# Attention and two MoE layers on one core: the bias table row by row, own buffers for one pass, and new planner costs

## The chip, the cores and the metric

The kernel runs on one core of one Trainium2 chip. Its time is the device time of one execution in microseconds (us); lower is better. The core has TensorE (PE) for matmuls, VectorE (DVE), ScalarE (ACT), GpSimd (POOL), and SyncE (SP), whose queue issues most of the DMAs. Each engine works through its own queue in order and waits on semaphores for the others.

## The reference, cut to what matters

```
B, H, S, D = 4, 8, 576, 64
scores = q @ k.T / sqrt(D)                       # per batch and head
x      = log1p(|i - j|) / log1p(max(i, 1))       # i, j: positions
bias   = maximum(x * w1 + b1, 0) @ w2            # S x S x H, the same for every batch
attn   = softmax(scores + bias[h]);  o = attn @ v
x      = o as [2304, 512]
h      = max(x @ w1, x @ w2, x @ w3);  x = h @ w_out          # first MoE,  d_ff  768
out    = (sigmoid(x @ w_gate) * (x @ w_val)) @ w_out          # second MoE, d_ff 1536
```

Inputs and outputs are float32; the MoE weights come in as 64-bit floats and are decoded on the chip. The kernel splits numbers into a high and a low float16 part and makes three matmuls (high-high, high-low, low-high) of one product.

## The kernel before

**Bias.** The table of all biases, bias_d, lies in device memory, [H, S, S + 64] in float32, head by head. It is made in 36 groups of 16 rows (`bias_rows`): four hidden tiles on ACT or DVE, 16 small matmuls, an eviction on ACT or DVE (`copy_psum`, L574 and L575) into one of three staging buffers, and one store of 320 KB on the SP queue (L661). Partition p of a staging buffer holds one row of one head, row by row and in a row head by head.

**Attention.** `pair(P, it)` works on heads 2P and 2P + 1 (modulo 8) of batch P // 4 and on query block it: 128 rows each for it = 0 to 3 and 64 rows for it = 4. It loads the biases of these rows and the two heads (L815 on SP or L816 on ACT), makes the scores (L804, L807), adds and takes the maximum on DVE (L820), and the exponential on ACT (L821). `by_pe` normalizes on POOL (L831) or DVE (L832) and transposes on PE (L836); `by_dma` does it by DMA transposes (L847). `value_out` multiplies with v (L863). In the first batch the loop goes over query blocks outside and heads inside, and the remaining bias groups are made in between: after the first query block 24 of the 36 groups are recorded, after the second 32, after the third all. So the bias stage and the first batch of attention run together.

**First MoE.** `moe1(b)` makes the products of batch b with three weight matrices (L914). For batch 0 it goes in two passes, over tokens 0 to 255 and 256 to 575. In a pass it goes through the three matrices, and in each through six columns of 128 features. A column is 12 matmuls into one of two PSUM banks in turn (`mm_0`, banks 6 and 7). A column of the first matrix is evicted into one of six column buffers `hms` (L574, L575), those of the second and third take the maximum with it (L944), and after the third the buffer is split into hT (L950, L951). The first three `hms` lie in the room `hm_f` of tile wm, the second three in tile x, at X2[:, 5760:6912]. The weights are read and decoded by a side job (`first_weights`): loads L674, decode in three DVE steps (L536 to L538), split into float16 on ACT (L684) and DVE (L685). For the output weights its raw buffers are X2[:, 3072:4608] and X2[:, 4608:6144] in turn.

**Second MoE.** After attention, its weights and staging take over the room of tile am (`attic`), and L914 and L1179 fill PE to the end.

**Order.** Everything is first recorded, with the regions that it reads and writes, and then `emit` plans one order for each engine: a list scheduler with a window per engine, four classes of priority (bias and MoE evictions first, then attention, the MoE, preparations) and an estimate of each instruction's duration (`cost`). An item that may run on two engines goes where it would end first. The planner follows every region exactly; for its dependences on the chip, the framework below it finds them again by its own means and puts in the semaphore waits. The order in a queue is then fixed.

Of the kernel before, what the change touches and what calls it, by code (L numbers as in the profile page):

```python
# [10 lines left out]
F32 = mybir.dt.float32  # L11
# [110 lines left out]
class Recorder:  # L122
# [8 lines left out]
    def __init__(self, nc, untracked):  # L131
        self.nc = nc
        self.untracked = untracked
        self.items, self.first = [], 0
        self.mem = Mem()
        self.cls = 0
        self.joined = None
        self.t_eng = {e: 0.0 for e in self.WINDOW}
        self.busy = {e: 0.0 for e in self.WINDOW}
        self.t_dma = 0.0  # L140
        self.bank = {i: {} for i in range(8)}
        self.log = []
        self.passed = {e: False for e in self.WINDOW}
        for attr, eng in self.ENGINES.items():
            setattr(self, attr, Engine(self, getattr(nc, attr), eng))
# [51 lines left out]
    @staticmethod  # L197
    def cost(eng, method, out, reads, kwargs):

        n = 1  # L200
        for _, c in out.ap[1:]:
            n *= c
        parts = out.ap[0][1]
        psum = any("PSUM" in str(a.space) for a in reads)
        if method.startswith("dma"):
            if "transpose" in method:
                return 1.33 if n > 1200 else 1.0 + 0.0003 * n, 0.12 + 0.00141 * n, 1.6
            dram = "DRAM" in str(out.space)
            if dram:
                n, parts = 1, 1  # L210
                for _, c in out.ap:
                    n *= c
            size = n * parts * (4 if "32" in str(out.dtype) else 2)
            return (0.45 if eng == "SP" else 0.1), size / (285e3 if dram else 400e3 if size > 6e5 else 300e3) * (1.6 if parts == 64 and n > 500 else 1.0) + 0.03, 1.85
        if eng == "PE":
            f32 = "float32" in str(reads[0].dtype)
            if method == "transpose":
                return 0.045 + 0.00055 * n, 0.0, 0.22
            if n <= 8:
                return 0.142, 0.0, 0.22  # L220
            t = (max(n / 2400, 0.03) + 0.0023) * (4 if f32 else 1)
            if kwargs.get("tile_position") is not None:
                depth = reads[0].ap[0][1]
                t *= (depth if depth < 128 else parts) / 128
                t += 0.012 if f32 else 0.008 if depth < 128 else 0.004
                if n <= 64:
                    t += 0.012
            return t, 0.0, 0.22
        vec = any(isinstance(kwargs.get(x), bass.AP) for x in ("scale", "bias")) or any(a.ap[-1][1] == 1 and n > 8 for a in reads)
        if eng == "DVE":  # L230
            half = "16" in str(out.dtype) and all("16" in str(a.dtype) for a in reads)
            if n <= 8:
                return (0.1 if n <= 2 else 0.13), 0.0, 0.12
            add = 0.07 if vec else 0.0
            t = {"tensor_tensor_reduce": 0.07 + 0.00105 * n, "scalar_tensor_tensor": 0.055 + 0.00107 * n + add,
                 "tensor_scalar": 0.07 + add + 0.00104 * n if psum or half else 0.03 + 0.0006 * n + add, "tensor_tensor": 0.065 + 0.00106 * n,
                 "tensor_copy": 0.08 + (0.00063 if not psum else 0.00105) * n, "memset": 0.1 + 0.0005 * n}[method]
            return t, 0.0, 0.12
        if eng == "ACT":
            t = (0.08 if psum else 0.19 if method != "copy" else 0.1) + (0.09 if psum and vec else 0.0) + 0.00083 * n  # L240
            return t + (0.09 if "accum_out" in kwargs and vec else 0.01), 0.0, 0.14
        t = {"tensor_tensor": 0.3 + 0.002 * n, "tensor_scalar": 0.08 + 0.00112 * n, "tensor_copy": 0.08 + 0.00112 * n}.get(method, 0.1 + 0.003 * n)
        if method == "tensor_scalar" and kwargs.get("op1") == ALU.max:
            t = 2.2
        return t, 0.0, 0.12

    def start(self, it, e):

        t = self.t_eng[e]
        for d in it.deps:  # L250
            e2, lat, own = self.ends[d]
            x = own if e2 == e == "PE" else lat
            if x > t:
                t = x
        for i in it.banks:
            for o, x in self.bank[i].items():
                if o != e and x > t:
                    t = x
        return t

    def choose(self, e, lists, force=False):
# [31 lines left out]
    def emit(self):  # L293

        items, by_k = self.items, {it.k: it for it in self.items}
        self.ends = getattr(self, "ends", {})
        lists = {e: [[] for _ in range(self.NCLS)] for e in self.WINDOW}
        for it in items:
            it.left = 0
            for d in it.deps:  # L300
                if d in by_k:
                    by_k[d].users.append(it)
                    it.left += 1
            for e in it.alts:
                lists[e][it.cls].append(it)
        left = len(items)
        picks = {}
        stale = set(lists)
        while left:
            for e in stale:  # L310
                picks[e] = self.choose(e, lists)
            cand = [(p[0], e) for e, p in picks.items() if p]
            if not cand:
                picks = {e: self.choose(e, lists, True) for e in lists}
                cand = [(p[0], e) for e, p in picks.items() if p]
            s, e = min(cand)
            it = picks[e][1]
            calls, (busy, work, lat) = it.alts[e]
            self.t_eng[e] = s + busy
            self.busy[e] += busy  # L320
            if work:
                self.t_dma = max(self.t_dma, s + 0.3) + work
                f = self.t_dma + lat
                self.ends[it.k] = (None, f, f)
            else:
                self.ends[it.k] = (e, s + busy + lat, s + busy)
                for i in it.banks:
                    self.bank[i][e] = s + busy + lat
            self.log.append((s, busy, e, it.k, it.cls))
            it.done = True  # L330
            left -= 1
            stale = set(it.alts) | {e}
            for u in it.users:
                u.left -= 1
                if not u.left:
                    stale |= set(u.alts)
            stale |= {o for o in lists if self.passed[o] or picks[o] and (len(picks[o][1].alts) > 1 or picks[o][1].banks & it.banks)}
            for o, ks in lists.items():
                if o in stale:
                    for c in range(self.NCLS):  # L340
                        if ks[c] and ks[c][0].done:
                            ks[c] = [x for x in ks[c] if not x.done] if len(ks[c]) < 64 else self.trim(ks[c])
            for c in calls:
                c()
        self.first += len(items)
        self.items = []
# [91 lines left out]
def tile_kernel(ctx, tc, q, k, v, w1, b1, w2, mw1, mw2, mw3, mwo, gw, vw, ow, xtab, masks, out):  # L438
    B, H, S, D = q.shape
# [6 lines left out]
    HS, SB = S // 2, S + 64  # L446
# [6 lines left out]
    junk = const.tile([128, 768], BF16, tag="junk", name="junk")  # L453
    nc = Recorder(tc.nc, {x.tensor.name for x in (junk[:, :], q, k, v, w1, b1, w2, mw1, mw2, mw3, mwo, gw, vw, ow, xtab, masks, out)})

    bias_d = dram.tile([H, S, SB], F32, tag="bias_d", name="bias_d")
    PS = psum.tile([128, 4096], F32, tag="ps", name="ps")

    def bank(i, n=512, at=0):
# [8 lines left out]
    Am = arena.tile([128, NA], F32, tag="am", name="am")  # L468
# [3 lines left out]
    def take(mem, n):  # L472
        a = free[id(mem)]
        free[id(mem)] = a + n
        return mem[:, a:a + n]

    def ring(mem, count, n, view=lambda x: x):
        return Ring([view(take(mem, n)) for _ in range(count)])
# [22 lines left out]
    ph_at = free[id(Am)]  # L501
    ph_r = ring(Am, 2, 2 * S, lambda t: t.bitcast(F16).rearrange("p (a s) -> p a s", a=2))
    e_r = ring(Am, 2, 2 * S)
    PT0 = take(Am, 2304)
    PT1 = take(Am, 2880)
    pt0 = PT0.rearrange("p (t s) -> p t s", t=9)
# [135 lines left out]
    def bias_rows(ti):  # L642
# [15 lines left out]
        m_ = msk[:, 4 + ti:5 + ti]  # L658
        copy_psum(bsb[:, 64:576], bo, m_)
        copy_psum(bsb.rearrange("p (a s) -> p a s", a=2)[:, :, 0:64], bt.unsqueeze(1).to_broadcast([128, 2, 64]), m_)  # L660
        nc.sync.dma_start(bias_d[:, 16 * ti:16 * ti + 16, :].rearrange("h i j -> i h j"), bsb[:, 0:SB])  # L661


    def first_weights(mats, raw, home, squares):
# [144 lines left out]
    def pair(P, it):  # L809

        m, h0 = rows[it], 2 * P % H
        e, l, r, bt = e_r(), l_r(), r_r(), bias_r()
        src = bass.AP(tensor=bias_d.tensor, offset=(h0 * S + 128 * it) * SB + 64, ap=[[SB, m], [S * SB - 64, 2], [1, S]])
        with nc.join():
            nc.sync.dma_start(bt[:m].rearrange("p (o s) -> p o s", o=2), src)  # L815
            nc.scalar.dma_start(bt[:m].rearrange("p (o s) -> p o s", o=2), src)  # L816
# [112 lines left out]
    def moe1(b, xd, mm):  # L929
# [27 lines left out]

        if b == 0:
            mm_0 = [mm, mm]
            hms = [t[:, 320 * i:320 * (i + 1)] for t in (hm_f, X2[:, 5760:6912]) for i in range(3)]  # L960
            for hf in range(2):
                for wi in range(3):
                    for m in range(K1):
# [278 lines left out]
```

## Time and profile before

| | us |
|---|---|
| median of 3 runs | 1083.62 |
| lowest, highest | 1081.85, 1084.55 |
| the profiled execution | 1084.82 |
| its span, first to last instruction | 1083.0 |
| PE busy | 1019.7 (94%) |
| DVE busy | 635.3 (59%) |
| ACT busy | 552.3 (51%) |
| POOL busy | 130.3 (12%) |
| mean granted TensorE clock | 0.979 |

Busy is the time in which an engine runs at least one instruction. The granted clock is the share of TensorE's full clock, 2.4 GHz; the lower of its two levels is 1.2 GHz. In the views an instruction is named by its line (L914), and tiles by their names without numbers: am, wm and x are the three large on-chip rooms, ps is PSUM, bias_d the table in device memory. A wait is put down to what released it last.

### The profile page before, as it was taken

How to read it: one execution, taken by the hardware profiler on the slowest of the kernel's cores; microseconds unless marked ns; L12 is line 12 of the kernel's file. 1: busy time of each engine (PE TensorE's matmuls, PEld its weight loads, DVE VectorE, ACT ScalarE, POOL GpSimd, SP SyncE). 2: the span in 40 equal slices, each digit the busy share in tenths (PEclk: the TensorE clock that was granted, in tenths of full speed). 3: DMA queues.
4: the chain of work that ended last, by engine and by line, in shares of the span. 5: the costliest groups of instructions: out<-in, count | busy, mean ns of one | idle time of the engine just before them, and what ended most of it. 6: DMA issues, size and time to landing. Idle time of an engine off the chain costs nothing.

```text
span 1083.0 us, 20927 instructions
## 1 busy us (share of the span) xinstructions
PE 1019.7 (94%) x8232; PEld 685.9 (63%) x8232; DVE 635.3 (59%) x1576; ACT 552.3 (51%) x1159; POOL 130.3 (12%) x159
## 2 busy tenths in 40 slices
PE   5877897799999999999999999999999999999998
PEld 2343465466566666676678777777765666776643
DVE  5866887788787887878899947922221221212210
ACT  6877896678788877777666426522110111211100
POOL 1011223503120422211110000000000000000000
PEclk9989898889999999999999999999999999999999
DMA  7767675978998989969855421000000000000001
GB/s 224 210 202 232 209 221 167 246 162 197 228 232 184 234 220 203 206 136 237 160 162 156 154 81 40 20 2 1 10 11 21 19 10 10 11 11 10 11 20 39
DMA packets 181133, 132.96 MB, mean 123 GB/s; under 512 B 123308, under 2 KB 152236, under 8 KB 181036
## 3 DMA queue, kind: packets, MB, share of 16 engines
q1 hardware_dynamic: 177364, 124.26, 46.0%
q10 hardware_dynamic: 3672, 7.38, 2.3%
q8 instruction: 64, 1.05, 0.4%
q14 instruction: 33, 0.27, 0.1%
HBM read 89.53 MB, written 16.52 MB: 98 GB/s over the span
## 4 chain that ended last, share of the span: by engine, by line
PE 79%; DVE 8%; DMA 6%; ACT 4%; issue 2%; POOL 1%; SPq 0%; ACTq 0%; POOLq 0%; DVEq 0%
PE ps L914 46%; PE ps L1179 13%; PE ps L863 6%; PE ps L804 4%; PE ps L836 4%; PE ps L650 2%; DMA bias_d<-am 2%; PE ps L807 2%; DMA am<-in_q_dram 1%; DVE am L820 1%; ACT am L574 1%; POOL am L831 1%; DMA am<-am 1%; PE ps L548 1%; DVE wm L944 1%
## 5 line engine op out<-in xcount | busy, mean ns | idle before, releaser
L914 PE MATMUL ps<-wm 128*128 128x320 f16 (+2 forms) x2304 | 305.1, 286 | 3.3 <-DVE wm L944 2.9
L914 PEld LDWEIGHTS <-am 128*128 128x128 f16 x2304 | 225.5, 98 | 58.8
L914 PEld LDWEIGHTS <-wm 128*128 128x128 f16 x2304 | 222.8, 99 | 60.3 <-issue 8.8
L914 PE MATMUL ps<-x,am 128*128 128x288 f16 x1728 | 214.3, 286 | 0.0
L821 ACT ACTIVATE am<-am,small 128x576 f32<-128x576 f32 (+1 forms) x160 | 123.0, 770 | 43.9 <-DVE small L820 37.7
L1179 PE MATMUL ps<-wm 128*128 128x512 f16 x648 | 142.0, 379 | 0.0
L1153 DVE SCALAR_TENSOR_TENSOR wm<-ps,wm 128x576 f32<-128x576 f32 x48 | 36.4, 757 | 161.6 <-PE ps L914 160.4
L820 DVE CUSTOM_DVE_ANT_0 am<-ps,am 128x576 f32<-128x576 f32 (+1 forms) x160 | 117.6, 748 | 22.4 <-issue 5.5
L1150 ACT ACTIVATE wm<-ps,ug 128x576 f32<-128x576 f32 x48 | 35.6, 741 | 155.0 <-PE ps L914 154.8
L1179 PEld LDWEIGHTS <-wm 128*128 128x128 f16 x648 | 63.4, 98 | 74.0
L1154 ACT CAST wm<-wm 128x576 f16<-128x576 f32 x48 | 32.2, 671 | 129.4 <-DVE wm L1153 129.4
L863 PE MATMUL ps<-am 128*64 128x320 f16 (+3 forms) x1000 | 88.4, 323 | 6.9 <-DVE small L594 4.5
L831 POOL TENSOR_SCALAR am<-am,small 128x576 f32<-128x576 f32 (+1 forms) x73 | 70.2, 971 | 198.1 <-DVE small L823 118.5
L836 PE MATMUL ps<-ident,am 128*128 128x128 f32 x396 | 66.5, 290 | 11.1 <-POOL am L831 7.5
L914 PE MATMUL ps<-am 128*128 128x288 f16 x576 | 71.2, 286 | 0.0
L574 ACT ACTIVATE am<-ps 128x512 f32<-128x512 f32 (+3 forms) x128 | 58.5, 473 | 15.3 <-PE ps L836 13.8
L1184 DVE TENSOR_TENSOR am<-ps,uo 128x512 f32<-128x512 f32 x16 | 11.1, 692 | 93.3 <-PE ps L1179 93.3
L845 DVE SCALAR_TENSOR_TENSOR am<-am,small 128x576 f16<-128x576 f32 (+1 forms) x72 | 59.2, 847 | 10.3 <-ACT am L844 9.7
L836 PEld LDWEIGHTS ps<-ident,am 128*128 128x128 f32 x396 | 45.7, 146 | 28.2 <-POOL am L831 15.3
L804 PE MATMUL ps<-am 64*128 64x512 f16 (+1 forms) x390 | 57.0, 389 | 3.2 <-DVE small L820 3.1
L581 ACT ACTIVATE junk<-am 128x640 bf16<-128x640 f32 (+1 forms) x72 | 48.8, 678 | 20.2 <-DVE am L538 8.9
L863 PEld LDWEIGHTS ps<-am 128*64 128x64 f32 x640 | 41.9, 150 | 22.7 <-issue 8.9
(148 smaller groups left out, 1181.1 us busy)
## 6 DMA issues: line engine op xcount, KB each, us to landing
am<-bias_d SPq DMA_DIRECT2D x52, 576.0 KB, 4.4
bias_d<-am SPq DMA_DIRECT2D x36, 320.0 KB, 3.5
wm<-in_moe_w_dram SPq DMA_DIRECT2D x12, 768.0 KB, 5.5
am<-bias_d ACTq DMA_DIRECT2D x12, 576.0 KB, 4.4
am<-in_moe_w_gate_dram SPq DMA_DIRECT2D x12, 512.0 KB, 4.6
am<-in_moe_w_val_dram SPq DMA_DIRECT2D x12, 512.0 KB, 4.6
am<-in_moe_w_out_dram SPq DMA_DIRECT2D x12, 512.0 KB, 3.4
out_dram<-am SPq DMA_DIRECT2D x36, 128.0 KB, 2.3
```

The lines of the kernel that those rows point to most:

```text
L574: nc.scalar.activation(dst, src, AF.Copy, scale=scale)
L581: nc.scalar.activation(junk[:, 0:n], src, AF.Square, accum_out=acc)
L804: nc.tensor.matmul(s_main[o][:m], lhsT=q_[h, eq], rhs=k_[h, ek, 0:512], start=(i == 0), stop=(i == 2), tile_position=(64 * o, 0))
L820: nc.vector.tensor_tensor_reduce(e[:m, c], S_[o][:m], bt[:m, c], -1.0, 3.0e38, ALU.add, ALU.min, mx[:m])
L821: nc.scalar.activation(e[:m, c], e[:m, c], AF.Exp, scale=-1.0, bias=mx[:m], accum_out=l[:m, o:o + 1])
L831: nc.gpsimd.tensor_scalar(e[:m, c], e[:m, c], r[:m, o:o + 1], 1.0, op0=ALU.mult, op1=ALU.mult)
L836: nc.tensor.transpose(ps[:, t], e[:, 128 * (t0 + t):128 * (t0 + t) + 128], ident)
L845: nc.vector.scalar_tensor_tensor(ph[:m, 1, c], e[:m, c], f, ph[:m, 0, c], op0=ALU.mult, op1=ALU.subtract)
L863: nc.tensor.matmul(ps[64 * o:64 * o + 64, :N], lhsT=vv[:, o, tv], rhs=pp[:, tb], start=(i == j == 0), stop=(i == len(todo) - 1 and j == 4) ...
L914: nc.tensor.matmul(ps, lhsT=W(wp, kk), rhs=X(xp, kk), start=(first and i == 0), stop=(last and i == 2))
L1153: nc.vector.scalar_tensor_tensor(hm3(sg), pv, DOWN2, hm3(sg), op0=ALU.mult, op1=ALU.mult)
L1179: nc.tensor.matmul(po, lhsT=gT[:, gi, kk, 128 * ct:128 * ct + 128], rhs=OW[:, wi, kk], start=(kk == 0 and i == 0), stop=(kk == K2 - 1 and ...
```

## The change

Three things are changed together. The bias table becomes [S, H, S + 64]: row by row, the eight heads of a row side by side, so that a store is one contiguous block, and a load reads for each row one run of 1152 values over two neighbouring heads. (In a table row the 64 places at one end are a copy, so that the even head is read from place 64 and the odd head from place 0.) The second three column buffers of the first MoE's first batch get 960 columns of their own in tile am, ahead of the two buffers of transposed probabilities, which move up. And the planner's durations are set anew: DMA transposes and SP's issue of a DMA take longer, PE's small products and POOL's scaling too, and a DMA can start no earlier than the eighth DMA before it has landed.

```diff
+        self.lanes = [0.0] * 8
...
-                return 1.33 if n > 1200 else 1.0 + 0.0003 * n, 0.12 + 0.00141 * n, 1.6
+                return (1.55 if n > 1200 else 1.1 + 0.0003 * n), 0.12 + 0.00141 * n, 1.6
...
-            return (0.45 if eng == "SP" else 0.1), size / ...
+            return (0.55 if eng == "SP" else 0.1), size / ...
...
-                t += 0.012 if f32 else 0.008 if depth < 128 else 0.004
+                t += 0.012 if f32 else 0.012 if depth < 128 else 0.006
...
-        t = {..., "tensor_scalar": 0.08 + 0.00112 * n, "tensor_copy": 0.08 + 0.00112 * n}...
+        t = {..., "tensor_scalar": 0.09 + 0.0014 * n, "tensor_copy": 0.09 + 0.0014 * n}...
...
+        if it.alts[e][1][1]:
+            t = max(t, self.lanes[0])
...
+                self.lanes = self.lanes[1:] + [f]
...
-    bias_d = dram.tile([H, S, SB], F32, tag="bias_d", name="bias_d")
+    bias_d = dram.tile([S, H, SB], F32, tag="bias_d", name="bias_d")
...
+    hm_x = take(Am, 960)
     PT0 = take(Am, 2304)
...
-        nc.sync.dma_start(bias_d[:, 16 * ti:16 * ti + 16, :].rearrange("h i j -> i h j"), bsb[:, 0:SB])
+        nc.sync.dma_start(bias_d[16 * ti:16 * ti + 16].rearrange("i h j -> (i h) j"), bsb[:, 0:SB])
...
-        src = bass.AP(tensor=bias_d.tensor, offset=(h0 * S + 128 * it) * SB + 64, ap=[[SB, m], [S * SB - 64, 2], [1, S]])
+        src = bass.AP(tensor=bias_d.tensor, offset=(128 * it * H + h0) * SB + 64, ap=[[H * SB, m], [SB - 64, 2], [1, S]])
...
-            hms = [t[:, 320 * i:320 * (i + 1)] for t in (hm_f, X2[:, 5760:6912]) for i in range(3)]
+            hms = [t[:, 320 * i:320 * (i + 1)] for t in (hm_f, hm_x) for i in range(3)]
```

## Rows read from the trace of the kernel before

**Rows 1.** Windows by stretch: busy us (x instructions) of each engine, clock, DMA.

```profile
core 0: us, PE busy (x) PEld busy (x) DVE busy (x) ACT busy (x) POOL busy (x), PEclk, DMA share, GB/s
0.00:40.00 40.00, 24.69 (x243) 12.44 (x243) 26.00 (x67) 27.41 (x46) 4.47 (x14) 0.96 0.81 228
40.00:166.00 126.00, 106.57 (x1087) 56.96 (x1086) 94.60 (x250) 101.26 (x218) 23.44 (x27) 0.93 0.70 216
166.00:226.00 60.00, 44.53 (x347) 27.60 (x345) 45.71 (x131) 37.84 (x96) 23.32 (x24) 0.80 0.68 175
226.00:613.00 387.00, 379.06 (x3268) 266.88 (x3266) 325.79 (x844) 285.43 (x639) 77.58 (x94) 1.00 0.85 196
613.00:1083.00 470.00, 464.80 (x3296) 321.99 (x3296) 143.19 (x287) 100.38 (x164) 1.53 (x1) 1.00 0.08 22
```

**Rows 2.** Chain of waits, 40 to 110 us: shares by line, then start, us, what.

```profile
by line: DMA bias_d<-am 23.5%; PE ps L650 15.9%; ACT am L574 11.6%; PE ps L863 6.9%; DMA am<-in_k_dram 6.0%; issue 5.8%; DMA am<-bias_d 5.4%; ACT am L821 4.8%; PE ps L836 3.9%; PE ps L654 2.3%; ACT am L640 2.3%; PE ps L593 2.2%; PE ps L804 
...
48.85 3.13 DMA bias_d<-am
...
51.99 3.78 DMA am<-bias_d
...
55.85 3.09 DMA bias_d<-am
```

**Rows 3.** Waits of the SP queue, 40 to 166 us: total us, times, longest.

```profile
SPq L661 <- DMA am<-bias_d: 41.3, 11, 7.7
SPq L815 <- DMA bias_d<-am: 28.1, 12, 3.7
```

**Rows 4.** Waits of the engines, 40 to 166 us.

```profile
ACT am L574 <- DMA bias_d<-am: 12.7, 6, 3.3
PE ps L650 <- ACT am L574: 10.4, 8, 3.5
```

**Rows 5.** Stores before 40.5 us by line, and the SP queue's timeline.

```profile
L661 SPq DMA_DIRECT2D bias_d<-am x8: 542/548/649, 15.1 to 35.1; - x8
...
164.15 0.59 SPq L661 DMA_DIRECT2D bias_d<-am  x1
168.55 1.27 SPq L815 DMA_DIRECT2D am<-bias_d  x2
```

**Rows 6.** Windows of line L914 alone: PE, PEld, clock, DMA.

```profile
100.00:166.00 66.00, 8.87 (x60) 5.29 (x60) 0.95 0.73 230
166.00:226.00 60.00, 0.00 (x0) 0.00 (x0) 0.80 0.68 175
```

**Rows 7.** Line L574, 95 to 250 us: ns min/median/max, first and last start.

```profile
L574 ACT ACTIVATE wm<-ps,small x3: 476/477/485, 143.8 to 150.4; 128x256 f32<-128x256 f32 x3
L574 ACT ACTIVATE x<-ps,small x3: 467/475/475, 220.1 to 227.6; 128x256 f32<-128x256 f32 x3
```

**Rows 8.** Timeline of DVE: start, us, instruction, count.

```profile
219.18 1.80 DVE L538 SCALAR_TENSOR_TENSOR x<-x 128x768 int32<-128x768 int32 x2
```

**Rows 9.** Timeline of ACT: the last split of the second and the third matrix.

```profile
162.58 0.92 ACT L684 ACTIVATE wm<-wm,small 128x768 f16<-128x768 f32 x1
...
193.32 1.76 ACT L684 ACTIVATE wm<-wm,small 128x768 f16<-128x768 f32 x2
```

**Rows 10.** Timeline of PE: 69 matmuls of the first pass.

```profile
227.51 7.69 PE L914 MATMUL ps<-wm 128*128 128x256 f16 x69
```

**Rows 11.** Groups by line, 40 to 226 us: busy us, mean ns, idle before.

```profile
L831 POOL TENSOR_SCALAR am<-am,small 128x576 f32<-128x576 f32 (+1 forms) x37 | 38.2, 1042 | 113.5 <-DVE small L823 74.9 <-PE ps L836 13.3 <-ACT am L574 9.0
L832 DVE TENSOR_SCALAR am<-am,small 128x576 f32<-128x576 f32 (+1 forms) x7 | 3.6, 517 | 0.2
```

**Rows 12.** Timeline of the SP queue: three bias loads and a weight load.

```profile
169.86 0.59 SPq L674 DMA_DIRECT2D wm<-in_moe_w_dram  x1
170.55 15.50 SPq L815 DMA_DIRECT2D am<-bias_d  x3
```

More of the change, by code (lines that the diff above doesn't have):

```diff
@@ L213, in cost @@
             size = n * parts * (4 if "32" in str(out.dtype) else 2)
-            return (0.45 if eng == "SP" else 0.1), size / (285e3 if dram else 400e3 if size > 6e5 else 300e3) * (1.6 if parts == 64 and n > 500 else 1.0) + 0.03, 1.85
+            return (0.55 if eng == "SP" else 0.1), size / (285e3 if dram else 400e3 if size > 6e5 else 300e3) * (1.6 if parts == 64 and n > 500 else 1.0) + 0.03, 1.85
         if eng == "PE":
@@ L241, in cost @@
             return t + (0.09 if "accum_out" in kwargs and vec else 0.01), 0.0, 0.14
-        t = {"tensor_tensor": 0.3 + 0.002 * n, "tensor_scalar": 0.08 + 0.00112 * n, "tensor_copy": 0.08 + 0.00112 * n}.get(method, 0.1 + 0.003 * n)
+        t = {"tensor_tensor": 0.3 + 0.002 * n, "tensor_scalar": 0.09 + 0.0014 * n, "tensor_copy": 0.09 + 0.0014 * n}.get(method, 0.1 + 0.003 * n)
         if method == "tensor_scalar" and kwargs.get("op1") == ALU.max:
@@ L336, in emit @@
                     stale |= set(u.alts)
-            stale |= {o for o in lists if self.passed[o] or picks[o] and (len(picks[o][1].alts) > 1 or picks[o][1].banks & it.banks)}
+            stale |= {o for o in lists if self.passed[o] or picks[o] and (len(picks[o][1].alts) > 1 or picks[o][1].banks & it.banks or work and picks[o][1].alts[o][1][1])}
             for o, ks in lists.items():
```

## The prediction

> **What bounds the kernel now.** I read the windows by stretch first, then the chain of waits and the wait lists of the stretches that are not full, and last the timelines of the lines that the diff touches.
>
> The windows [rows 1] cut the span in five. From 226 us on TensorE (PE) is busy for 379.06 of 387 us and then for 464.80 of 470 us, at a granted clock of 1.00: together 13.1 us are idle, and what shortens that part is less matmul work left to do in it. Before 226 us PE is idle for 15.3 us (0 to 40), 19.4 us (40 to 166) and 15.5 us (166 to 226), and the granted clock is 0.96, 0.93 and 0.80. So a gain must come from the first 226 us: a stage there gets shorter, or matmuls of the later, full part are done in its gaps.
>
> From 40 to 110 us the chain of waits is not on an engine for much of the time: 23.5% of these 70 us is the store into bias_d and 5.4% the load from it, 16.4 and 3.8 us [rows 2]. The reader sees them take turns: the store issued at 48.85 lands before the load at 51.99 goes, and the next store at 55.85 goes when that load has landed. The SP queue's waits say the same: stores waited 41.3 us for loads, loads 28.1 us for stores [rows 3]. By 40.5 us eight stores are out [rows 5]. A store holds 16 rows of the table, so these are rows 0 to 127, all that the first four loads (attention's first query block) read. The third load, at 51.99, therefore waits for a store of rows it does not read. The addresses explain it: head by head, a store touches its 16 rows in all eight heads, so its span from first to last address covers nearly the whole table and meets the span of every load, although few bytes are shared. That it is the span which makes the wait is my inference; the trace shows only the wait.
>
> From 166 to 226 us no matmul of the MoE line L914 runs at all, after 60 in the stretch before [rows 6]. Sixty is five columns of twelve (4 chunks times 3 products). Three of them are evicted into wm at 143.8 to 150.4, the next three go into x at 220.1 to 227.6 [rows 7], and the third and fourth decode of the output weights, in x, end only then: two last steps from 219.18, 1.80 us together, so the third ends at about 220.1, just ahead of the first eviction into x at 220.15 [rows 8]. The fourth and fifth column buffers (X2 from 5760 on) overlap the second raw weight buffer (X2 4608 to 6144). Two finished columns thus sit in the only two PSUM banks of this pass for about 57 us and shut out every later one.
>
> **The change part by part.**
>
> *Bias table row by row.* No instruction is added: 36 stores and 80 loads stay. A store is now one contiguous block of 16 rows, and a load of query block i lies within that block's rows, so spans of different blocks no longer meet. What goes is bounded above by the chain's 16.4 + 3.8 = 20.2 us and below by nothing (the waits move to other engines in the same queue order). Between them I take what reached PE: in 40 to 166 us ACT's eviction waited 12.7 us for stores to land, and PE waited 10.4 us for those evictions [rows 4]. I take **10.4 us**. What is late next is real: the load at 168.55 follows the last store, issued at 164.15, because it reads those rows [rows 5]; making the bias rows then runs at the pace of ACT and DVE, busy for 101.26 and 94.60 of 126 us [rows 1]. Ready loads would otherwise save at most the 3.8 us of load on the chain, which is counted already. A load becomes one run of 4608 bytes per partition instead of two of 2304; no row has such a load alone, its nearest is the same load at 3.8 us on the chain, so I price the layout's effect on transfer time at 0, with 1 us either way.
>
> *Own room for the column buffers.* The second three buffers move to am, and the wait for the output weights' decode goes. What can run in its place: the second weight matrix is split by 162.58 + 0.92 = 163.5, the third by 195.1 [rows 9]. From 163.5 on, the sixth column of the first matrix and six of the second can run: 7 x 12 = 84 matmuls. Sixty-nine of the same shape took 7.69 us at full clock, 111 ns each [rows 10], so 84 make **9.4 us**, which fit in the 15.5 us of idle time. Six more of the third matrix (72 matmuls, 8.0 us) could follow after 195; with them it would be 17.4 us, more than there is idle time, so the upper bound is 15.5 us. The lower is 0, if the columns land where PE is busy anyway. Their evictions, some 0.48 us each [rows 7], are moved and not added: 7 x 0.48 = 3.4 us over ACT and DVE, idle for 22.2 and 14.3 us there [rows 1]. If that cover were gone it would cost those 3.4 us. am grows by 960 columns, which shifts the two probability buffers against the last stage's weight room; PE is full there, and I price it at 0.
>
> *The planner's costs.* They change the order alone. The largest moves GpSimd's scaling: 37 instructions took 38.2 us, seven on DVE 3.6 us [rows 11]. If all 37 went to DVE it would carry 37 x 0.517 = 19.1 us more beside 31.4 + 14.3 = 45.7 us idle; if they stay, nothing. A DMA that the planner now holds until the eighth before it has landed is issued later than planned before. The transposes and SP's issue are priced higher, so SP's list (bias loads and stores, weights, q, k, v, transposes in one queue) is shuffled as well. The nearest row for what one misplaced item costs is the SP queue's stretch of three bias loads from 170.55, 15.5 us long [rows 12]. I take 0, with 15.5 us either way as bounds.
>
> **A rule weighed.** Where PE pauses, the granted clock falls: 0.80 in 166 to 226 us [rows 1], which between 1.2 and 2.4 GHz means 40% of that time at the lower level. The Trainium skill (TensorE: Matmul & The Clock Gate, "What's actually happening") says that the throttled state is the default and that activity releases it. By that rule the added columns would also speed up the matmuls already there: the sum would be lower by up to half of 40% of 44.53 us, 8.9 us; by the trace alone, which shows low clock beside gaps but no cause, it is 0.
>
> **The sum.** The profiled execution took 1084.82 us (span 1083.0 and 1.8 around it), 1.2 us over the median of 1083.62. 1084.82 - 10.4 - 9.4 = 1065.0, and against the median 1063.8: I predict **1064 us**.
>
> **Rivals.**
> - *Better than forecast.* The whole chain share goes, the idle time in 166 to 226 is filled, and PE runs at full clock: 1083.6 - 20.2 - 15.5 = 1047.9, and with the 8.9 us of clock 1039. For it: the columns are ready to run and evict to free engines. Against: ACT is at 80% already, and the real wait on the last rows stays. Chance 0.18.
> - *One of the two does nothing.* Either the stores and loads still wait for each other (the wait was by tensor, not by address span): 1083.6 - 9.4 = 1074. Or the columns' gain is given back when the second batch's attention cannot feed PE: 1083.6 - 10.4 = 1073. For the first: no row shows how the span is compared. Against the second: DVE is idle for 61 of 387 us after 226 [rows 1]. Chance 0.22; both at once, no change, 0.08.
> - *Slower.* In the new order the third matrix's load, now at 169.86 between bias loads, falls behind such a stretch of bias loads that wait for buffers [rows 12], at 170.55. W3's split then comes 15.5 us later and DVE and PE stand before it in their queues; PE stays idle for 15.5 us more, the columns' gain is lost, and two later batches meet a stretch like it once each, while the layout's gain stays: 1083.6 - 10.4 + 15.5 = 1088.7 with one, 1104 with two. It decides from the point where such stretches cost more than 19.8 us together. Against: the planner's durations come nearer to the rows (GpSimd's 1.03 us each against 0.73 assumed before for 576 elements). Chance 0.12.
>
> **How the numbers follow.** The forecast (1055 to 1072) has 0.40. A measurement of this kernel tells about 0.3%, 3.3 us, from no change. Faster is 0.40 + 0.18 + 0.22 = 0.80, the same 0.08, slower 0.12. The range runs from 1043 (most of the better case) to 1084 (it leaves out the slower one and a part of no change).
>
> **What would show it.** Right: in the SP queue's waits the stores' wait for bias_d loads falls from 41.3 us to a few, and ACT's evictions no longer wait for stores; L914 has 84 or more matmuls between 160 and 220 us, and no eviction waits for the decode into x; PE's idle time before 226 us falls from 50 us to about 30, and from the end of attention's first batch to the end of the span little changes. Wrong: L661 still waits for loads; PE idle reappears between 226 and 613 us, above all where the first MoE ends; or DVE and ACT are full before 166 us while PE waits for them.

## The result, and the profile after

The changed kernel takes 1049.36 us (median of 4 runs, 1047.94 to 1050.35) against 1084.09 us in the same comparison; the ratio is 0.9673, 95% interval 0.9640 to 0.9707. That is 34.7 us less, where 20 were forecast: inside the range, but below the 1055 to 1072 around the sum. Lines 140 and up have moved by up to five: L919 is the MoE's matmul line L914 of before, L666 the store L661, L820 the load L815, L579 ACT's eviction L574, L836 GpSimd's scaling L831.

The windows by stretch answer to [rows 1]; the columns are the same.

```profile
0.00:40.00 40.00, 25.20 (x256) 11.21 (x256) 25.45 (x66) 27.78 (x46) 4.55 (x14) 1.00 0.79 233
40.00:166.00 126.00, 118.94 (x1273) 69.39 (x1274) 115.66 (x314) 114.70 (x253) 22.46 (x28) 1.00 0.74 240
166.00:226.00 60.00, 59.17 (x545) 41.89 (x543) 58.32 (x150) 46.66 (x106) 15.38 (x19) 1.00 0.80 199
226.00:613.00 387.00, 372.57 (x3166) 262.76 (x3165) 321.88 (x838) 272.32 (x611) 69.14 (x80) 0.98 0.86 193
613.00:1046.00 433.00, 427.92 (x2999) 292.78 (x2996) 122.00 (x234) 90.72 (x145) 0.00 (x0) 1.00 0.06 15
```

From 40 to 226 us PE's idle time fell from 34.9 to 7.9 us and the granted clock rose to 1.00. In the same 186 us DVE now does 174.0 us of work instead of 140.3, ACT 161.4 instead of 139.1: more of the first batch is behind it at 226 us. The fourth stretch has got worse, 14.4 us idle for 7.9. In all PE is idle for 42.3 us instead of 63.3, and busy for 1003.8 us instead of 1019.7 with the same 8232 matmuls, so 21.0 us are closed gaps and 15.9 us shorter matmuls; together that is the span's 36.9.

The SP queue's waits from 40 to 166 us answer to [rows 3] (total us, times, longest).

```profile
SPq L666 <- ACT am L579: 37.1, 20, 3.4
SPq L820 <- DVE small L825: 25.0, 7, 6.8
```

Stores and loads now wait for the other side for 0.9 us in all, before for 69.4; a store waits for its own eviction instead. All 36 stores are out by 141.9 us, before by 164.2 [rows 5] (line L666: ns min/median/max, first and last start).

```profile
L666 SPq DMA_DIRECT2D bias_d<-am x36: 319/327/1291, 14.2 to 141.9; - x36
```

The MoE line and its evictions answer to [rows 6, 7]: 281 matmuls run where none ran, and the second three buffers, now in am, are filled from 142.6 us on.

```profile
40.00:166.00 126.00, 16.50 (x117) 11.04 (x118) 1.00 0.74 240
166.00:226.00 60.00, 38.35 (x281) 26.86 (x279) 1.00 0.80 199
```

```profile
L579 ACT ACTIVATE wm<-ps,small x6: 468/493/528, 121.8 to 196.6; 128x256 f32<-128x256 f32 x3, 128x320 f32<-128x320 f32 x3
L579 ACT ACTIVATE am<-ps,small x6: 469/499/512, 142.6 to 205.0; 128x256 f32<-128x256 f32 x3, 128x320 f32<-128x320 f32 x3
```

### The profile page after: what moved, and what is told of

The parts are those of the page before. It is cut to its first block, busy times and chain, and to the rows that moved or that the text cites. A ratio compares the mean times of both kernels' runs of the same rounds, so it can differ in the third digit from the quotient of the medians.

```text
span 1046.1 us, 20916 instructions
## 1 busy us (share of the span) xinstructions
PE 1003.8 (96%) x8232; PEld 678.0 (65%) x8232; DVE 643.3 (61%) x1598; ACT 552.2 (53%) x1158; POOL 111.5 (11%) x138
## 4 chain that ended last, share of the span: by engine, by line
PE 59%; DVE 3%; ACT 2%; DMA 1%; issue 1%; POOL 0%; ACTq 0%; DVEq 0%; POOLq 0%
PE ps L919 40%; PE ps L1184 13%; PE ps L868 2%; PE ps L809 2%; PE ps L841 1%; PE ps L553 1%; DMA am<-bias_d 1%; PE ps L812 1%; DVE am L543 0%; DVE wm L949 0%; ACT junk L586 0%; DVE am L542 0%; ACT am L826 0%; DVE am L850 0%; DVE am L541 0%
## 5 line engine op out<-in xcount | busy, mean ns | idle before, releaser
L919 PE MATMUL ps<-wm 128*128 128x320 f16 (+2 forms) x2304 | 306.0, 286 | 0.9 <-DVE wm L874 0.7
L919 PEld LDWEIGHTS <-am 128*128 128x128 f16 x2304 | 225.5, 98 | 58.8
L919 PEld LDWEIGHTS <-wm 128*128 128x128 f16 x2304 | 222.7, 99 | 55.5 <-issue 3.8
L919 PE MATMUL ps<-x,am 128*128 128x288 f16 x1728 | 214.2, 286 | 0.0
L1155 ACT ACTIVATE wm<-ps,ug 128x576 f32<-128x576 f32 x48 | 35.6, 741 | 155.0 <-PE ps L919 154.8
L868 PE MATMUL ps<-am 128*64 128x320 f16 (+3 forms) x1000 | 81.8, 310 | 2.2 <-DVE wm L874 1.4
L836 POOL TENSOR_SCALAR am<-am,small 128x576 f32<-128x576 f32 (+1 forms) x53 | 50.3, 953 | 209.4 <-DVE small L828 102.1
L919 PE MATMUL ps<-am 128*128 128x288 f16 x576 | 71.2, 286 | 0.0
L841 PE MATMUL ps<-ident,am 128*128 128x128 f32 x396 | 64.0, 285 | 6.2 <-POOL am L836 3.3
L579 ACT ACTIVATE am<-ps 128x512 f32<-128x512 f32 (+2 forms) x130 | 58.8, 475 | 16.2 <-PE ps L841 13.4
L1160 DVE TENSOR_TENSOR wm<-wm 128x576 f16<-128x576 f32 x48 | 36.4, 758 | 29.3 <-ACT wm L1159 29.3
```

The source lines that it names most:

```text
L579: nc.scalar.activation(dst, src, AF.Copy, scale=scale)
L836: nc.gpsimd.tensor_scalar(e[:m, c], e[:m, c], r[:m, o:o + 1], 1.0, op0=ALU.mult, op1=ALU.mult)
L841: nc.tensor.transpose(ps[:, t], e[:, 128 * (t0 + t):128 * (t0 + t) + 128], ident)
L868: nc.tensor.matmul(ps[64 * o:64 * o + 64, :N], lhsT=vv[:, o, tv], rhs=pp[:, tb], start=(i == j == 0), stop=(i == len(todo) - 1 and j == 4) ...
L919: nc.tensor.matmul(ps, lhsT=W(wp, kk), rhs=X(xp, kk), start=(first and i == 0), stop=(last and i == 2))
```

## The experiments

Theory: the table frees the chain of stores and loads, the room frees the blocked banks, the planner's costs do little. The main rivals: the planner's order brings the time, and the room's gain is given back later. Each kernel is the kernel before with the named edits; times are medians beside runs of the kernel before on the same chip. The last four columns of the table come from one profiled execution of each kernel.

| kernel | us | ratio to before, 95% interval | PE idle 40 to 226 | PE idle 226 to 613 | DVE busy 40 to 226 | clock 40 to 226 |
|---|---|---|---|---|---|---|
| before | 1083 to 1085 | | 34.9 | 7.9 | 140.3 | 0.89 |
| table (a_rows) | 1067.9 | 0.986 [0.981, 0.992] | 22.2 | 7.9 | 158.9 | 0.94 |
| table in five pieces (t_blocks) | 1066.5 | 0.984 [0.981, 0.987] | 21.1 | 9.1 | 159.3 | 0.94 |
| room (b_room) | 1083.2 | 0.999 [0.996, 1.002] | 29.2 | 18.6 | 137.5 | 0.92 |
| costs (c_costs) | 1071.5 | 0.989 [0.984, 0.993] | 33.8 | 2.7 | 151.6 | 0.93 |
| limit alone (l_lanes) | 1071.5 | 0.988 [0.984, 0.991] | 31.4 | 4.0 | 153.8 | 0.94 |
| durations alone (d_dur) | 1072.3 | 0.987 [0.984, 0.991] | 30.6 | 7.7 | 155.0 | 0.92 |
| null draw 1 (n1_sp) | 1085.1 | 1.001 [0.999, 1.003] | 38.9 | 6.7 | 138.8 | 0.91 |
| null draw 2 (n2_pe) | 1079.2 | 0.996 [0.994, 0.998] | 39.3 | 5.5 | 141.6 | 0.93 |
| table, null draw 1 (an1) | 1062.0 | 0.981 [0.978, 0.984] | 24.8 | 6.3 | 160.5 | 0.96 |
| table, room (ab) | 1064.3 | 0.982 [0.977, 0.986] | 14.9 | 19.7 | 159.4 | 0.99 |
| room, costs (bc) | 1070.5 | 0.986 [0.983, 0.990] | 22.4 | 14.8 | 155.0 | 0.96 |
| table, costs (ac) | 1052.1 | 0.971 [0.966, 0.975] | 18.6 | 3.2 | 172.9 | 0.96 |
| all three | 1049.4 | 0.967 [0.964, 0.971] | 7.9 | 14.4 | 174.0 | 1.00 |

**The table alone.**

```diff
-    bias_d = dram.tile([H, S, SB], F32, tag="bias_d", name="bias_d")
+    bias_d = dram.tile([S, H, SB], F32, tag="bias_d", name="bias_d")
```

with the store and the load as in the change.

> Only the bias table row by row; buffers and planner durations as before. My theory: the table's layout frees the loop of stores and loads and is worth about half of the change or more, 10 to 22 us (1062 to 1074), the last bias store goes about 20 us earlier than 164 us, and L914 still has no matmul between about 145 and the decode into x, so its gap in PE stays. Rival 1 (planner): the new durations bring the time and the layout alone gives under 5 us (above 1079). Rival 2 (both are needed): the bias stage ends earlier but PE then waits longer for the column buffers, and the time is within 3 us of before.

Measured: 1067.9 us. The planner sees exact regions, so the order on PE and DVE is the same, instruction for instruction; only the waits differ, and the gain of some 16 us is theirs alone or the shapes'. The SP queue's waits, 40 to 166 us:

```profile
SPq L661 <- ACT am L574: 37.6, 19, 5.7
SPq L815 <- DVE small L820: 16.2, 6, 5.5
SPq L815 <- DMA bias_d<-am: 6.4, 1, 6.4
```

The stores' 41.3 us of waiting for loads are gone but for 0.6 us, and of the loads' 28.1 us one real wait of 6.4 us stays. PE's wait for ACT's eviction falls from 10.4 us [rows 4] to 1.0 us in this profile:

```profile
PE ps L650 <- ACT am L574: 1.0, 3, 0.6
```

The last store goes at 141.8 us, 22 us earlier, as expected. The MoE line L914 still has its gap, but the gap ends sooner, at 205.3 us instead of 226.1.

**Spans or shapes.** The table stays head by head, in five pieces of memory:

```diff
-    bias_d = dram.tile([H, S, SB], F32, tag="bias_d", name="bias_d")
+    bias_b = [dram.tile([H, rows[i], SB], F32, tag=f"bias_d{i}", name=f"bias_d{i}") for i in range(NIT)]
...
-        nc.sync.dma_start(bias_d[:, 16 * ti:16 * ti + 16, :].rearrange("h i j -> i h j"), bsb[:, 0:SB])
+        nc.sync.dma_start(bias_b[ti // 8][:, 16 * (ti % 8):16 * (ti % 8) + 16, :].rearrange("h i j -> i h j"), bsb[:, 0:SB])
...
-        src = bass.AP(tensor=bias_d.tensor, offset=(h0 * S + 128 * it) * SB + 64, ap=[[SB, m], [S * SB - 64, 2], [1, S]])
+        src = bass.AP(tensor=bias_b[it].tensor, offset=h0 * m * SB + 64, ap=[[SB, m], [m * SB - 64, 2], [1, S]])
```

> The kernel before with the table still head by head, but in five pieces of memory, one for each query block, so that the store's and load's shapes stay (runs of 2560 and two runs of 2304 bytes) and only the overlap of address spans across blocks goes. My theory: the waits of stores for loads go from 41 us to under 5 and the time is that of the row by row table, 1064 to 1072. Rival: a good part of that gain came from the contiguous shapes (shorter issue and transfers), and this kernel comes to 1074 to 1080.

Measured: 1066.5 us, the same as row by row within both intervals, with the same order of PE. Its waits of the SP queue, 40 to 166 us, have no wait of a store for a load:

```profile
SPq L661 <- ACT am L574: 32.5, 16, 6.8
SPq L815 <- DVE small L820: 13.6, 6, 6.4
SPq L815 <- DMA bias_d<-am: 6.0, 2, 5.7
```

So the gain is the end of waits between query blocks. The contiguous shapes add nothing that can be measured, although SP issues them sooner (below).

**The room alone.**

```diff
+    hm_x = take(Am, 960)
     PT0 = take(Am, 2304)
...
-            hms = [t[:, 320 * i:320 * (i + 1)] for t in (hm_f, X2[:, 5760:6912]) for i in range(3)]
+            hms = [t[:, 320 * i:320 * (i + 1)] for t in (hm_f, hm_x) for i in range(3)]
```

> Only the own room for the second three column buffers; table and durations as before. My theory: L914 runs 84 or more matmuls between 160 and 226 us, the granted clock there rises from 0.80 to 0.95 or more, and the time falls by 9 to 20 us (1064 to 1075), while the stores wait for bias loads as before (about 41 us from 40 to 166 us). Rival: the columns only move into places where PE was busy, under 4 us (above 1080).

Measured: no difference, 1083.2 us. That is the rival's number, but not for the rival's reason. The columns do run in the gap: from 166 to 226 us there are 171 matmuls of the MoE line (L915 here), PE is idle for 5.7 us instead of 15.5, and the clock is 0.91, a little under the 0.95 expected.

```profile
166.00:226.00 60.00, 54.29 (x529) 40.10 (x525) 47.80 (x141) 40.39 (x101) 21.77 (x24) 0.91 0.61 171
```

The gain is lost again 80 us later. The profiled execution is the slowest of ten, 1090.2 us, so it shows where the gain goes and not the exact balance of the median. These are windows of the kernel before, the same windows with the room, and then PE's timeline with the room (start, us, instruction, count, idle before and what ended it):

```profile
300.00:325.00 25.00, 25.00 (x220) 17.27 (x219) 21.09 (x55) 20.52 (x50) 5.60 (x8) 1.00 1.02 233
325.00:350.00 25.00, 23.41 (x209) 16.21 (x208) 17.70 (x50) 21.36 (x48) 2.60 (x3) 1.00 0.93 192
```

```profile
300.00:325.00 25.00, 19.78 (x166) 12.54 (x166) 19.52 (x51) 21.53 (x49) 8.17 (x10) 0.93 0.94 203
325.00:350.00 25.00, 18.48 (x116) 10.97 (x115) 16.78 (x45) 14.94 (x34) 6.67 (x8) 0.73 0.83 197
```

```profile
300.98 4.74 PE L915 MATMUL ps<-wm 128*128 128x288 f16 x39
307.32 0.49 PE L915 MATMUL ps<-wm 128*128 128x256 f16 x3
310.48 0.77 PE L837 MATMUL ps<-ident,am 128*128 128x128 f32 x5 [2.67 <-ACT am L575]
311.84 1.12 PE L837 MATMUL ps<-ident,am 128*128 128x128 f32 x4 [0.60 <-ACT am L575]
319.49 2.38 PE L864 MATMUL ps<-am 128*64 128x256 f32 x20 [0.88 <-DVE wm L870]
```

The output product of batch 0 (288 wide) ends at 305.7 us; the next batch's columns (256 wide) have their last input only after the last pair's first `value_out` (L864 at 319.5). Between them PE has attention alone and waits 11.7 us in these two windows, where the kernel before waited 1.6 us (300 to 350), and the clock falls to 0.73. PE's gap was moved, not closed.

**Table and room.** Both edits.

> The row by row table and the own room together, durations as before. My theory: the two gains add up to most of the change, 1048 to 1058, PE idle before 226 us about 25 us and a granted clock near 1.00 from 40 us on. Rival: without the new durations 10 us or more are missing against the changed kernel (above 1060).

Measured: 1064.3 us, the rival's number: 15 us are missing against the changed kernel. PE's idle time from 40 to 226 us is down to 14.9 us, and that from 226 to 613 us up to 19.7.

**The planner's costs alone**, both kinds of them, as in the change.

> Only the planner's durations and the limit of eight DMAs; table and buffers as before. My theory: the order changes little where it matters, within 6 us of before either way (1078 to 1090), since the false waits and the blocked banks stay. Rival: the new order is worth a third or more of the change, 12 us or more (below 1072).

Measured: 1071.5 us, 12 to 14 us faster; the rival holds and the theory falls. The stores still wait 35.8 us for loads, so this is another gain than the table's. In this profile PE idles 7.6 us less over the whole span, 5.2 us of it after 226 us, and is busy for 4.5 us less.

**The costs, taken apart**: only the limit of eight DMAs (`lanes`), and only the durations.

> The kernel before with the planner's limit of eight DMAs in flight alone, no other cost changed. Of the new costs (13.7 us together) my theory gives the larger share, 7 us or more, to this limit, since DMA landings pace the bias stage (1072 to 1079). Rival: the limit seldom binds and this kernel is within 4 us of before (above 1081).

> The kernel before with the new durations alone (transposes, SP's issue, small products, GpSimd's scaling), without the limit of eight DMAs. By my theory 0 to 7 us are gained here (1078 to 1086), with some 10 of GpSimd's 37 scalings before 226 us moved to DVE. Rival: this is where the gain of the costs lies, 9 us or more (below 1076).

Measured: 1071.5 and 1072.3 us. Each alone brings what both bring, so both of my expectations missed: the durations were to bring 0 to 7 us, and the limit the larger share. That looks like an order before that was drawn badly, so that any new one is better; two kernels with meaningless changes test it.

**Null draws.**

```diff
-            return (0.45 if eng == "SP" else 0.1), size / ...
+            return (0.46 if eng == "SP" else 0.1), size / ...
```

```diff
-                return 0.045 + 0.00055 * n, 0.0, 0.22
+                return 0.046 + 0.00055 * n, 0.0, 0.22
```

> The kernel before with one planner cost moved by a meaningless amount (SP's issue 0.46 us for 0.45), so that the order is drawn anew with nothing better known. The limit alone, the durations alone and both together each gave 12 to 14 us. My theory now: these gains are the price of the order before, a poor draw, and any new draw gains 6 us or more (1070 to 1078). Rival: the better durations themselves bring it, and this order is within 4 us of before (above 1080).

> The kernel before with another meaningless move (a PE transpose 1 ns longer): a second draw. Same theories: poor draw before, 1070 to 1078; better durations, above 1080. Draws that lie 10 us apart would say that no single one of these orders tells what a cost is worth.

Measured: 1085.1 and 1079.2 us, though the two orders differ from the one before at some 2000 and 1700 of PE's 8232 matmuls. A new draw is worth 0 to 5 us here, and the three informed orders 12 to 14. Both draws lie above the 1078 us that the poor draw allowed, the second between it and the rival's 1080. My theory of the poor draw falls, as far as two draws can tell. The windows show what the informed orders have in common; 40 to 226 us, of null draw 1 and then of the costs:

```profile
40.00:226.00 186.00, 147.10 (x1421) 82.97 (x1422) 138.82 (x377) 138.73 (x312) 45.41 (x48) 0.91 0.68 204
```

```profile
40.00:226.00 186.00, 152.19 (x1479) 87.78 (x1472) 151.64 (x410) 143.96 (x321) 35.99 (x38) 0.93 0.73 212
```

In the same time DVE does 12.8 us and ACT 5.2 us more work, and GpSimd ten instructions less. PE's waits for GpSimd's scaling, 40 to 613 us, in null draws 1 and 2, then in the costs and in the limit alone:

```profile
PE ps L836 <- POOL am L831: 11.9, 14, 2.6
```

```profile
PE ps L836 <- POOL am L831: 14.7, 15, 3.6
```

```profile
PE ps L840 <- POOL am L835: 3.7, 7, 1.4
```

```profile
PE ps L840 <- POOL am L835: 5.6, 9, 1.5
```

Against the costs' 3.7 us the null draws lose 8 to 11 us more there, the order before (7.5 us in the same list) 3.8 us. Against the kernel before, this wait is thus a small part of the 12 to 14 us. And the limit alone, which has the old duration for GpSimd, has less of this wait too, and so which cost does it is not settled; each duration by itself was not tried.

**Table with null draw 1.**

> The row by row table with the meaningless move of SP's issue cost (0.46 for 0.45). The table alone has the order of before and gave 1068, table and new costs 1052. If the new costs' gain is a better draw, this comes to 1052 to 1060; if the durations themselves bring it, to 1064 to 1072.

Measured: 1062.0 us, between the two expectations: by the medians the null draw is worth some 6 us here (the two intervals overlap), and the informed costs (next) 10 us more.

**All but the room; all but the table.**

> The changed kernel without the own room (row by row table and new planner costs). The single parts gave 1068 (table), 1083 (room) and 1071.5 (costs) against 1085 before; table and room 1064. My theory now: table and costs add up nearly, the room's gain is given back where the first MoE runs out ahead of the second batch's attention, so this kernel comes to 1050 to 1057, with no gap of PE at 275 to 350 us. Rival: the three need each other and without the room 10 us or more are missing against the changed kernel (above 1060).

> The changed kernel with the table head by head as before (own room and new planner costs). My theory: the stores and loads of bias_d wait for each other as before (35 to 41 us), and the time is that of the costs alone or a little better, 1064 to 1073. Rival: with the room's columns in place and better durations the waits of stores cost little, below 1058.

Measured: 1052.1 and 1070.5 us, both as the theory had it. The room is worth 2.8 us in the full change by these medians, and the intervals of the two ratios overlap, so that it may be nothing. The gap that it fills is also shorter by then: with the table and the costs alone the decode into x comes sooner, the first eviction into x starts at 194.2 us instead of 220.1 [rows 7], and 178 matmuls of the MoE line run from 166 to 226 us.

```profile
L578 ACT ACTIVATE x<-ps,small x6: 459/500/527, 194.2 to 238.6; 128x256 f32<-128x256 f32 x3, 128x320 f32<-128x320 f32 x3
```

Windows of 275 to 325 us show where its gain goes, of the changed kernel and then of table and costs without the room:

```profile
275.00:300.00 25.00, 20.53 (x142) 11.98 (x142) 18.32 (x51) 18.50 (x42) 4.27 (x6) 0.74 0.84 195
300.00:325.00 25.00, 22.27 (x192) 14.21 (x190) 22.51 (x64) 19.08 (x43) 7.96 (x10) 1.00 1.04 230
```

```profile
275.00:300.00 25.00, 23.88 (x213) 16.03 (x212) 19.07 (x54) 19.82 (x46) 3.79 (x6) 1.00 1.05 224
300.00:325.00 25.00, 25.00 (x224) 17.15 (x223) 20.37 (x56) 21.50 (x48) 4.82 (x8) 1.00 0.96 222
```

## Why the prediction was partly right

- **Where the time would come from** was right: the first 226 us. PE idles 27.0 us less from 40 to 226 us, and the stretches after 226 us gave nothing.
- **The table: right in its mechanism, and nearly right in its gap.** The term was 10.4 us, from the wait that reached PE; alone the table measured about 16 us. The profiles divide that: with the table (span 1062.3 us) PE idles 12.4 us less than before, in five pieces (span 1066.0 us) 11.8 us, both near the term. The rest, 8.3 and 5.2 us, is less busy time for the same 8232 matmuls, beside a clock of 0.94 instead of 0.89 from 40 to 226 us. The sum had put the clock at 0. Such a split of single profiles is good to some 4 us only: null draw 1, as slow as before, is busy for 3.8 us less and idle for 3.9 us more. That the address span makes the wait was an inference. Row by row the table is still one tensor, and the waits are gone, so that a wait by tensor is ruled out; in the five pieces only the blocks' memory is apart and every shape is as before. How the comparison is made, no run shows.
- **The room: right up to 226 us, wrong in the sum.** The term of 9.4 us assumed that after 226 us PE would only have less to do. Alone it measured nothing and in the whole change at most a few us. The rival "given back when the second batch's attention cannot feed PE" is what happened, at 300 to 350 us in the kernel with the room alone, and at 275 to 325 us in the changed one. I had argued against it with DVE's 61 idle us of 387, a mean over a stretch; the pair-by-pair chain of attention does not run faster because DVE is idle on average.
- **The costs: wrong.** I took 0 with 15.5 us either way. They measured 12 to 14 us alone and 16 us beside the table. What the step lacked was any row that tells planned from actual; the rows that I had, GpSimd's 1.03 us against 0.73 assumed, were used against the slower rival only, and not in the sum.
- **The clock.** Before, PE's gaps lay beside a clock of 0.93 and 0.80; with the gaps closed it is 1.00, and the same matmuls are busy for 15.9 us less. By the rule of the Trainium skill (TensorE: Matmul & The Clock Gate, "What's actually happening"), that activity releases the throttle, the prediction's estimate of 8.9 us could have been added for 166 to 226 us alone; the trace agrees in direction, there and from 40 us on. The room alone shows both sides of it: the clock goes up where the columns went, to 0.91, and down to 0.73 where they are missing.

The gain can be followed step by step: first the table, then the costs beside it (span 1048.7 us), then the room. PE's idle time goes by -12.4, -9.2 and +0.6 us, its busy time by -8.3, -4.4 and -3.2 us. PE's busy time stands first in these page lines, of the table, the five pieces, table and costs, and all three:

```profile
PE 1011.4 (95%) x8232; PEld 682.0 (64%) x8232; DVE 635.5 (60%) x1576; ACT 552.8 (52%) x1159; POOL 134.4 (13%) x159
PE 1014.5 (95%) x8232; PEld 683.5 (64%) x8232; DVE 635.9 (60%) x1576; ACT 552.7 (52%) x1159; POOL 134.3 (13%) x159
PE 1007.0 (96%) x8232; PEld 677.7 (65%) x8232; DVE 643.7 (61%) x1603; ACT 550.0 (52%) x1158; POOL 104.1 (10%) x133
PE 1003.8 (96%) x8232; PEld 678.0 (65%) x8232; DVE 643.3 (61%) x1598; ACT 552.2 (53%) x1158; POOL 111.5 (11%) x138
```

The forecast of 1064 us is thus the sum of a table too small by 6, a room too large by 7 to 9, and costs too small by 12 to 16. Its two terms, 19.8 us, come near the 21.0 us of gaps that closed, but that is luck: 9.2 us of these came with the costs and none with the room, and the 15.9 us of shorter matmuls stand in no term. The better case, 1047.9 us, met the number with parts that do not hold: it had the room's 15.5 us and no gain from the costs.

## What to carry to other kernels

When a store and a load of different rows take turns in the trace, look at the address spans of the two accesses: lay the tensor out, or cut it, so that what is written and read at the same time does not interleave. Before filler work is moved forward into a gap, ask when its successor's inputs come; if they come no sooner, the gap is moved too. Where an order is planned by costs, bring them nearer to what the trace shows (here it paid, though by which cost is open), and measure a meaningless change of a cost beside it to know what a new draw alone is worth.

## What was not expected of the hardware

SP's own time to issue a store fell from 550 to 327 ns (median) when the store became one block, and in the five pieces, head by head, it stayed at 543 ns (line L661: ns min/median/max), of before, table and five pieces:

```profile
L661 SPq DMA_DIRECT2D bias_d<-am x36: 517/550/1494, 15.1 to 164.2; - x36
```

```profile
L661 SPq DMA_DIRECT2D bias_d<-am x36: 319/327/1202, 15.2 to 141.8; - x36
```

```profile
L661 SPq DMA_DIRECT2D bias_d<-am x36: 517/543/761, 15.2 to 142.3; - x36
```

The loads' issue went from 537 to 451 ns. The median time to landing did not fall with it (stores 3.5 us before, 4.2 by rows, 4.6 in pieces), and the two kernels take the same time.
